# Storing the factors with fewer transfers, v's parts from ScalarE, and sums in pieces of 16 tokens

## The chip, the cores and the metric

The kernel runs on one core of a Trainium2 chip. The metric is the device time of one execution in microseconds (us). A span is the time from the first to the last instruction of the program in a profiled execution.

## The reference

Eight batches, eight heads, 576 tokens, head size 64, 32 memories a head. The first half compresses keys and values into memories and attends to them; the second routes the 128 best tokens of each batch through a two-layer network.

```python
a = phi - np.max(phi, axis=2, keepdims=True)          # phi: (b, h, s, m), softmax over the tokens s
a = np.exp(a)
a = a / (np.sum(a, axis=2, keepdims=True) + 1e-09)
k_m = np.einsum('bhsm,bhsd->bhmd', a, k)
v_m = np.einsum('bhsm,bhsd->bhmd', a, v)
scores = (1.0 / np.sqrt(q.shape[-1])) * np.matmul(q, k_m.transpose(0, 1, 3, 2))
attn = np.exp(scores - np.max(scores, axis=-1, keepdims=True))
attn = attn / (np.sum(attn, axis=-1, keepdims=True) + 1e-09)
x = np.matmul(attn, v_m)                              # then laid out as (b, s, 512)
scores = np.einsum('bsd,d->bs', x, w_gate)
out = x.copy()
for b in range(B):
    top_idx = np.argpartition(-scores[b], capacity)[:capacity]   # capacity = 128
    xe = x[b, top_idx]
    ye = np.maximum(xe @ w1, 0.0) @ w2                # 512 -> 1024 -> 512
    g = 1.0 / (1.0 + np.exp(-scores[b, top_idx]))
    out[b, top_idx] = x[b, top_idx] + g[:, None] * ye
```

Which tokens are chosen depends on the scores, so much of the arithmetic is carried out more exactly than fp32 instructions alone would do it: numbers are split into a high and a low part.

## The kernel before

**Groups and the softmax.** Heads are taken in 16 groups (batch, four heads): 4 x 32 memories fill the 128 partitions, and the 576 tokens lie along the free dimension. `softmax` runs one group through some 29 instructions of VectorE and 16 of ScalarE on tiles of 128 x 576; a `yield` cuts it into steps. Two channels (`ch` 0 and 1) with buffers of their own take turns through the first eight groups; the other eight run on channel 0 alone. Its last part, `keys`, transposes the factors a on TensorE (line 314), has ScalarE copy them out (316), splits them into `hi` and `lo` on VectorE (320, 322), stores both parts to a DRAM tensor `aparts` (325: eight transfers from POOL's queue, one for each part and head), and multiplies them with k (331).

**v.** `split_v` loads v of a group (whole groups in the first phase, halves later; line 291), splits it on VectorE (294, 296) and stores both parts to DRAM, `vparts`, each twice (298, from POOL's queue).

**The sums.** v_m is summed token by token in a fixed order. `all_sums` works on sets of two batches (four groups): a piece of `T` = 18 tokens is loaded back from DRAM with `load_rows`, one transfer for v (344) and four for a (351, one for each of the four heads), all from SyncE's queue, so that 32 partitions hold the combinations of parts; then 18 x 4 small products accumulate in PSUM (382). Three buffers `v_rows` and `a_rows` rotate. A set is 32 pieces, and there are four sets. The first piece of a set waits until the schedule's turn is at least five past that in which the set's last group was made (line 367).

**Attention and network.** `attention(b)` centres the memories (`centre`), computes scores (490) from a loaded q (108), exp and tanh of them (476 to 479), the attention sum (548), divides (552), adds the mean over the memories (555: on POOL while softmaxes are still under way, on VectorE after that), computes gate scores (520 to 525), stores x twice (560, 564), ranks the tokens (`rank`, 601) and gathers the chosen rows (630). `ffn` is the network (654, 664) and scatters the result (671). The next batch's q is loaded between scores and attention sum (683).

**The order.** The instruction order is written out by a loop over turns at the end of the function. Each turn takes one step of a softmax; every fourth turn (every second, once attentions run) one step of `split_v`; 7 steps of the sums before attentions run, 10 beside them and softmaxes, 12 after; one step of each live attention; and two of the network. A step of the sums is two tokens. Each engine executes its own instructions strictly in this order, and SyncE, ScalarE and POOL issue their transfers in it too. When channel 1 is through, its buffers are freed and new pools are opened, among them `vio2` for v's halves with one buffer.

Of the kernel before, what the change touches and what calls it, by code (L numbers as in the profile page):

```python
# [39 lines left out]
def kernel(  # L40
# [26 lines left out]
    F = w1.shape[1]  # L67
    KD, KF = D // P, F // P
    SET = 2
    T = 18  # L70
    scale = 1.0 / Dh ** 0.5
    out_flat = out.rearrange("b s d -> (b s) d")

# [28 lines left out]
    def load_k(i, ch):  # L102
        ks[i] = exs[ch].tile([PT, NC, D // NG], F32, name="kb")
        nc.sync.dma_start(out=ks[i], in_=k[groups[i]])
# [82 lines left out]
    def softmax(i, ch):  # L187

        ex = exs[ch]

        def t(name, dtype=F32):

            return ex.tile([P, NC * P if name in WIDE else S], dtype, name=name)[:, :S]

        r = phis.pop(i)
        less_mx = ex.tile([P, 1], F32, name="mx")
        nc.vector.tensor_scalar(out=t("den"), in0=r, scalar1=-1.0, scalar2=None, op0=ALU.mult,
                                op1=ALU.min, accum_out=less_mx)
        nc.scalar.activation(r, r, AF.Identity, bias=less_mx)
        q = t("q", I16)  # L200
        act(q, r, LOG2E)
        yield
        for ln2 in (LN2_HI, LN2_LO):
            stt(out=r, in0=q, scalar=-ln2, in1=r, op0=ALU.mult, op1=ALU.add)

        rh, rl = t("rh", I16), t("rl")
        act(rh, r, 2.0 ** 11)
        num, den = t("num"), t("den")
        act(num, r, SQ[0], SQ[1], AF.Square)
        act(den, r, EXP_Q[2] * UP, EXP_Q[1] * UP)  # L210
        ends = t("lo"), t("big")
        act(ends[0], rh, -0.2734375 * UP * GRID, UP)
        act(ends[1], rh, UP * GRID / 4, EXP_P[1] * UP)
        yield
        stt(out=num, in0=num, scalar=SQ[2], in1=r, op0=ALU.add, op1=ALU.mult)
        act(num, num, 1.0, EXP_P[2] * UP)
        stt(out=rl, in0=rh, scalar=-GRID, in1=r, op0=ALU.mult, op1=ALU.add)

        def near(val, f, end):


            low = t("low")
            stt(out=low, in0=val, scalar=-f * UP, in1=r, op0=ALU.add, op1=ALU.mult)
            stt(out=low, in0=rl, scalar=f * UP, in1=low, op0=ALU.mult, op1=ALU.add)
            tt(out=val, in0=end, in1=low, op=ALU.add)

        yield
        load_k(i, ch)
        near(den, -0.2734375, ends[0])
        dh = t("dh", I16)  # L230
        act(dh, den, FINE)
        near(num, 0.25, ends[1])
        vh = t("vh", I16)
        act(vh, num, GRID)
        y0 = t("y0", I16)
        act(y0, r, 1.0, 14 * LN2, AF.Exp)
        inv = t("rl2")
        act(inv, r, INV[0], INV[1], AF.Exp)
        act(inv, inv, 1.0, INV[2] - 9 * LN2, AF.Exp)
        yield  # L240


        lo, big, low = t("lo"), t("big"), t("low")
        tt(out=low, in0=num, in1=rl, op=ALU.mult)
        stt(out=lo, in0=num, scalar=GRID, in1=vh, op0=ALU.mult, op1=ALU.subtract)
        tt(out=lo, in0=lo, in1=rh, op=ALU.mult)
        tt(out=big, in0=vh, in1=rh, op=ALU.mult)
        tt(out=low, in0=low, in1=lo, op=ALU.add)
        stt(out=num, in0=big, scalar=UP, in1=low, op0=ALU.add, op1=ALU.add)
        yield  # L250

        dl, p = t("lo"), t("big")
        stt(out=dl, in0=den, scalar=FINE, in1=dh, op0=ALU.mult, op1=ALU.subtract)
        tt(out=p, in0=y0, in1=dh, op=ALU.mult)
        tt(out=num, in0=num, in1=p, op=ALU.subtract)
        tt(out=dl, in0=y0, in1=dl, op=ALU.mult)
        tt(out=num, in0=num, in1=dl, op=ALU.subtract)
        two_q = t("den", I32)
        yield
        act(two_q, q, UP, 127 * UP, AF.Relu)  # L260
        tt(out=num, in0=num, in1=inv, op=ALU.mult)
        tt(out=num, in0=num, in1=y0, op=ALU.add)
        sm = ex.tile([P, 4], F32, name="sm")
        e = num
        stt(out=e, in0=num, scalar=FINE, in1=two_q.bitcast(F32),
            op0=ALU.mult, op1=ALU.mult, accum_out=sm[:, 0:1])

        nc.vector.tensor_scalar_add(sm[:, 0:1], sm[:, 0:1], 1e-9)
        nc.vector.reciprocal(sm[:, 1:2], sm[:, 0:1])
        nc.vector.tensor_single_scalar(sm[:, 2:3].bitcast(I32), sm[:, 0:1].bitcast(I32), -4096,  # L270
                                       op=ALU.bitwise_and)
        nc.vector.tensor_sub(sm[:, 3:4], sm[:, 2:3], sm[:, 0:1])
        nc.vector.tensor_scalar_mul(sm[:, 2:3], sm[:, 2:3], -1.0)
        a0 = t("vh", F16)
        nc.scalar.activation(a0, e, AF.Copy, scale=sm[:, 1:2])  # L275
        yield
        for part in (2, 3):
            stt(out=e, in0=a0, scalar=sm[:, part:part + 1], in1=e, op0=ALU.mult, op1=ALU.add)
        stt(out=e, in0=e, scalar=sm[:, 1:2], in1=a0, op0=ALU.mult, op1=ALU.add)  # L279
        soft[i] = e  # L280
        yield
        yield from keys(i, ch)

    def split_v(some, pool, cuts):

        n = 4 * S * Dh // P
        for b, g in some:
            for x0 in range(0, n, n // cuts):
                x = slice(x0, x0 + n // cuts)
                vb = pool.tile([P, n // cuts], F32, name="vb")  # L290
                nc.sync.dma_start(out=vb, in_=v[b, g, :, x])
                yield
                hi = pool.tile([P, n // cuts], F32, name="vhi")
                nc.vector.tensor_single_scalar(hi.bitcast(I32), vb.bitcast(I32), -4096,
                                               op=ALU.bitwise_and)
                nc.vector.tensor_sub(vb, vb, hi)  # L296
                for vp, src in enumerate((vb, hi)):
                    nc.gpsimd.dma_start(  # L298
                        out=vparts[b, g, :, vp].rearrange("w r s d -> w (r s d)")
                                               .rearrange("w (p x) -> p w x", p=P)[:, :, x],  # L300
                        in_=src.unsqueeze(1).to_broadcast([P, 2, n // cuts]))
                yield
# [3 lines left out]
    def keys(i, ch):  # L306
# [13 lines left out]
        nc.vector.tensor_single_scalar(hi.bitcast(I32), aS.bitcast(I32), -4096,  # L320
                                       op=ALU.bitwise_and)
        nc.vector.tensor_sub(lo, aS, hi)  # L322
        for part, src in enumerate((lo, hi)):
            for h in range(4):
                nc.gpsimd.dma_start(  # L325
                    out=aparts[h, b, g, part].rearrange("(c p) m -> p c m", p=PT),
                    in_=src[:, :, h * M:(h + 1) * M])
        km = bank([P, 2, 2 * M])
        for rr in range(2):
            for c in range(NC):  # L330
# [3 lines left out]
        for u in range(2):  # L334
            part = slice(u * Dh, (u + 1) * Dh)
            nc.scalar.activation(kbd[b][part, 2 * g:2 * g + 2, u * M:(u + 1) * M],  # L336
                                 km[part, :, u * M:(u + 1) * M], AF.Copy)

    accs = [accp.tile([P, 512], F32, name=f"acc{i}") for i in range(2 * SET)]

    def load_rows(k, st, ch):
# [4 lines left out]
            in_=vparts[some].rearrange("b g t w r s d -> (b g t w r) (s d)")  # L346
                [:, ch * T * Dh:(ch + 1) * T * Dh])
        for h in range(4):
            src = aparts[h, some].rearrange("b g t s m -> (b g t) (s m)")
            src = src[:, ch * T * M:(ch + 1) * T * M]  # L350
            nc.sync.dma_start(  # L351
                out=a_rows[k % 3][2 * h::8, h].rearrange("p s m -> p (s m)").bitcast(F32),
                in_=src.unsqueeze(1).to_broadcast([4 * SET, 2, T * M]))

    def all_sums():
# [7 lines left out]
        def load_some(end):  # L363
            while len(loaded) < min(end, len(pieces)):
                st, ch = pieces[len(loaded)]

                if not all(turn >= made.get(i, turn) + 5
                           for i in range(st * SET * NG, (st + 1) * SET * NG)):
                    break
                load_rows(len(loaded), st, ch)  # L370
# [156 lines left out]
    def attend(b, general):  # L527
        eT, tg = eTs[b % 2], tgs[b % 3]
        row, rest = mean[b]
        for c0 in range(0, NT, 2):  # L530
# [5 lines left out]
                                     rhs=heads_of, start=True, stop=True)  # L536
            if working:
                yield
            rd = step.tile([P, 2, H], F32, name="rd")[:, :cols]
            nc.vector.tensor_scalar(out=rd.rearrange("p c (g h) -> p c g h", g=2), in0=den,  # L540
                                    scalar1=float(M), scalar2=1e-9, op0=ALU.add, op1=ALU.add)
# [2 lines left out]
            for c in range(cols):  # L544
                o = bank([P, D])
                nc.tensor.matmul(out=o, lhsT=ones3, rhs=rest, start=True, stop=False)
                for g in range(2):
# [4 lines left out]
                nc.vector.tensor_mul(x[:, c].rearrange("p (h d) -> p h d", d=Dh),  # L552
                                     o.rearrange("p (h d) -> p h d", d=Dh),
                                     rd[:, c].unsqueeze(2).to_broadcast([P, H, Dh]))
            (nc.gpsimd if working else nc.vector).tensor_add(  # L555
                x, x, row.unsqueeze(1).to_broadcast([P, cols, D]))
            yield
            score(tg[:, c0:c0 + cols, 1], x, cols)
# [117 lines left out]
    def attention(b, general=False):  # L676
# [2 lines left out]
        yield from (scores_less_max if general else scores)(b)  # L679
        for j in range(2):  # L680
            yield
            if not general and b + 1 < B:
                load_q(b + 1, j)
        yield from attend(b, general)
        yield
        yield from rank(b)
# [66 lines left out]
    while True:  # L753
# [6 lines left out]
        if working and next(working[0], working) is working:  # L760
            finish(working[1])
            working.clear()
        if working and turn % (2 if attend_all else 4) == 1:
            next(working[1], None)
        for _ in range(steps()):
            next(sums, None)
        if attend_all is None and set(order[1]) <= set(made):
# [4 lines left out]
                ctx.enter_context(tc.tile_pool(name=name, bufs=2 - (name == "one"),  # L772
                                               reuse_waits="tile"))
                for name in ("step", "work", "one"))
            vio = ctx.enter_context(tc.tile_pool(name="vio2", bufs=1, reuse_waits="tile"))
            working[1] = split_v(groups[two + 1:], vio, 2)
            for j in range(2):
                load_q(0, j)
# [58 lines left out]
```

## Time and profile before

| | us |
|---|---|
| median of three runs | 911.14 (907.17 to 918.13) |
| the profiled execution's own time | 899.93 |
| its span | 898.1 |
| PE, DVE, ACT, POOL busy | 584.2, 611.5, 295.3, 234.9 |
| mean granted TensorE clock | 0.822 |

PE is TensorE, DVE VectorE, ACT ScalarE, POOL GpSimd, SPq SyncE's queue, which only issues transfers and is never counted as busy. A busy time is the union of an engine's instructions. In the view of groups and lines, `xN` is a count, then busy us and mean ns of one, then the idle time of the engine ahead of them and what ended it. In the view of waits, a line reads: who waited, for whom, us in total, times, longest. In the view of one line's instructions, three durations in ns are shortest, median and longest.

The engines by 40 equal slices of the span, in tenths:

```
PE   0122322556764646695847889867889989888794
DVE  4899888857874765779789685979845333537820
ACT  3434434324441513332433624343331310332130
POOL 7033311330220432151423314232511010112200
DMA  6367936876857786788554778664256566123300
```

### The profile page before, as it was taken

Reading aid. Unit: us, or ns where it says so; the run is one execution under the profiler, and the core shown is the slowest. Engines: PE = TensorE matmul, PEld = TensorE weight load, DVE = VectorE, ACT = ScalarE, POOL = GpSimd, SP = SyncE. Lnnn points to the kernel's source line nnn. Section 1 sums busy time; section 2 is a strip of 40 time slices with the busy share of each in tenths; the row PEclk is TensorE's granted clock in tenths of the full one; section 3 lists DMA queues with packets and bytes.
Section 4 is the critical chain, followed back from the end, with each engine's and each line's share of the span. In section 5 each row is a group of like instructions: output and inputs, shape, how many; then the busy total and the mean of one; then the engine's idle time right before and its main releaser. Section 6 shows DMA issues by size and latency. Waiting matters only on the chain. (4 is left out here: it accounts for less than half of the span.)

```text
span 898.1 us, 25253 instructions
## 1 busy us (share of the span) xinstructions
PE 584.2 (65%) x10738; PEld 427.7 (48%) x10738; DVE 611.5 (68%) x1117; ACT 295.3 (33%) x578; POOL 234.9 (26%) x349
## 2 busy tenths in 40 slices
PE   0122322556764646695847889867889989888794
PEld 0012222456653535574714557555556577544441
DVE  4899888857874765779789685979845333537820
ACT  3434434324441513332433624343331310332130
POOL 7033311330220432151423314232511010112200
PEclk9999999757585776886667979985899977989597
DMA  6367936876857786788554778664256566123300
GB/s 169 144 198 271 312 124 204 274 250 176 253 154 241 231 259 186 254 289 254 181 186 139 221 210 256 201 191 138 71 171 195 181 202 204 58 77 117 117 25 15
DMA packets 61944, 166.10 MB, mean 185 GB/s; under 512 B 11136, under 2 KB 21376, under 8 KB 61824
## 3 DMA queue, kind: packets, MB, share of 16 engines
q1 hardware_dynamic: 40096, 94.14, 34.8%
q0 software_dynamic: 21728, 70.27, 23.7%
q8 instruction: 87, 1.43, 0.7%
q14 instruction: 33, 0.27, 0.1%
HBM read 96.21 MB, written 68.16 MB: 183 GB/s over the span
## 5 line engine op out<-in xcount | busy, mean ns | idle before, releaser
L382 PE MATMUL acc<-a_rows,v_rows 32*64 32x128 f32 x9216 | 214.3, 253 | 127.8 <-DMA a_rows<-aparts 121.4
L382 PEld LDWEIGHTS acc<-a_rows,v_rows 32*64 32x64 f32 x9216 | 193.5, 162 | 170.4 <-issue 83.0
L314 PE MATMUL bank<-ident,num 128*96 128x128 f32 x96 | 21.3, 386 | 104.4 <-DVE num L279 99.4
L331 PE MATMUL bank<-lo,kb 96*128 96x64 f32 x384 | 64.5, 345 | 20.0 <-ACT lo L316 20.0
L331 PEld LDWEIGHTS bank<-lo,kb 96*128 96x128 f32 x384 | 62.7, 257 | 25.5 <-ACT lo L316 22.4
L325 POOL DMA_DIRECT2D aparts<-low x64 | 46.9, 740 | 104.8 <-DVE low L322 89.7
L298 POOL DMA_DIRECT2D vparts<-vb x23 | 16.9, 735 | 217.8 <-DVE vb L296 217.8
L654 PE MATMUL bank<-w_sb,xeT 128*128 128x512 f32 x128 | 69.8, 679 | 4.9 <-ACT xeT L645 3.2
L314 PEld LDWEIGHTS bank<-ident,num 128*96 128x96 f32 x96 | 15.4, 178 | 108.8 <-issue 88.4
L664 PE MATMUL bank<-w_sb,hT 128*128 128x512 f32 x128 | 60.8, 609 | 0.0
L548 PE MATMUL bank<-vbd,eT 128*128 128x256 f32 x160 | 58.3, 499 | 0.0
L552 DVE TENSOR_TENSOR xj<-bank,rd 128x512 f32<-128x512 f32 x40 | 27.5, 688 | 32.9 <-PE bank L548 32.4
L601 DVE SCALAR_TENSOR_TENSOR cmp<-row,tg,wide 128x576 bf16<-128x576 f32 x40 | 32.5, 814 | 24.0 <-ACT row L587 23.1
L325 POOL DMA_DIRECT2D aparts<-big x64 | 46.5, 734 | 3.8 <-DMA vparts<-vhi 3.7
L548 PEld LDWEIGHTS bank<-vbd,eT 128*128 128x128 f32 x160 | 34.1, 236 | 16.0 <-issue 12.1
L654 PEld LDWEIGHTS bank<-w_sb,xeT 128*128 128x128 f32 x128 | 25.3, 215 | 30.6 <-issue 22.1
L275 ACT ACTIVATE vh<-num,sm 128x576 f16<-128x576 f32 x16 | 12.4, 776 | 78.2 <-DVE sm L270 63.1
L555 POOL TENSOR_TENSOR xj<-xj,mean 128x1024 f32<-128x1024 f32 (+1 forms) x11 | 23.6, 2147 | 49.5 <-DVE xj L552 41.6
L479 DVE SCALAR_TENSOR_TENSOR eT<-es,th 128x288 f32<-128x288 f32 x32 | 14.4, 450 | 31.9 <-ACT th L477 31.9
L664 PEld LDWEIGHTS bank<-w_sb,hT 128*128 128x128 f32 x128 | 22.5, 189 | 25.9 <-issue 24.4
L336 ACT ACTIVATE kbd<-bank 64x64 f32<-64x64 f32 x32 | 7.0, 218 | 83.5 <-PE bank L331 83.3
L560 POOL DMA_DIRECT2D out<-xj x24 | 16.3, 678 | 66.8 <-DVE xj L555 63.8
(149 smaller groups left out, 1155.8 us busy)
## 6 DMA issues: line engine op xcount, KB each, us to landing
v_rows<-vparts SPq DMA_DIRECT2D x128, 288.0 KB
a_rows<-aparts SPq DMA_DIRECT2D x512, 36.0 KB
vparts<-vb POOLq DMA_DIRECT2D x9, 1152.0 KB, 5.5
vparts<-vhi POOLq DMA_DIRECT2D x9, 1152.0 KB, 8.7
kb<-in_k SPq DMA_DIRECT2D x16, 576.0 KB
qb<-in_qT SPq DMA_DIRECT2D x16, 576.0 KB
out<-xj POOLq DMA_DIRECT2D x16, 512.0 KB, 4.1
xs<-xj POOLq DMA_DIRECT2D x16, 512.0 KB, 4.3
```

Source lines behind the costliest of these rows:

```text
L298: nc.gpsimd.dma_start(out=vparts[b, g, :, vp].rearrange("w r s d -> w (r s d)") .rearrange("w (p x) -> p w x", p=P)[:, :, x], in_=src.unsq ...
L314: nc.tensor.transpose(out=tp[:, c], in_=a[:, (c0 + c) * PT:(c0 + c + 1) * PT], identity=ident)
L325: nc.gpsimd.dma_start(out=aparts[h, b, g, part].rearrange("(c p) m -> p c m", p=PT), in_=src[:, :, h * M:(h + 1) * M])
L331: nc.tensor.matmul(out=km[:, rr], lhsT=kb[:, c, rr * P:(rr + 1) * P], rhs=aS[:, c, rr * 2 * M:(rr + 1) * 2 * M], start=(c == 0), stop=(c = ...
L382: nc.tensor.matmul(out=accs[i][:Dh, :P].rearrange("p (h m) -> p h m", m=M), lhsT=vr[p, s], rhs=ar[p, :, s], start=(ch == 0 and s == 0), st ...
L548: nc.tensor.matmul(out=o[:, g * 4 * Dh:(g + 1) * 4 * Dh], lhsT=eT[:, g, (c0 + c) * P:(c0 + c + 1) * P], rhs=vbd[b % 3][:, g], start=False, ...
L552: nc.vector.tensor_mul(x[:, c].rearrange("p (h d) -> p h d", d=Dh), o.rearrange("p (h d) -> p h d", d=Dh), rd[:, c].unsqueeze(2).to_broadc ...
L555: (nc.gpsimd if working else nc.vector).tensor_add(x, x, row.unsqueeze(1).to_broadcast([P, cols, D]))
L560: nc.gpsimd.dma_start(out=out[b, c0 * P:c0 * P + (cols - 1) * P + n].rearrange("(c p) d -> p c d", p=n), in_=x[:n])
L601: nc.vector.scalar_tensor_tensor(out=cmp, in0=row, scalar=g, in1=wide[:, off:off + S], op0=ALU.is_equal, op1=ALU.mult, accum_out=equal[:, ...
L654: nc.tensor.matmul(out=ps[:n], lhsT=xeT[:, d, :n], rhs=w1_sb[:, d, f0:f0 + 512], start=(d == 0), stop=(d == KD - 1))
L664: nc.tensor.matmul(out=ps[:n], lhsT=hT[:, f, :n], rhs=w2_sb[:, f], start=(f == 0), stop=(f == KF - 1))
```

## The change

It has these parts:

- A group's factors are stored by two POOL transfers, one for each part, in place of eight; `aparts` gets a layout in which a token block of 96 and a head are outer dimensions. The stores stand after the products with k in the text.
- A piece of the sums has 16 tokens in place of 18, since a piece must now lie inside a block of 96 tokens.
- v's parts are stored from ScalarE's queue, one step after VectorE has split them; v's halves get a second buffer; `split_v` takes a step in every third turn in the first phase, and in two of three later.
- The mean is added by VectorE throughout.
- k is loaded one step of the softmax later; the next batch's q is loaded inside the attention sum; the rows of a set are loaded four turns, not five, after its last group.

```diff
-    T = 18
+    T = 16
+    assert PT % T == 0
...
         yield
-        load_k(i, ch)
         near(den, -0.2734375, ends[0])
...
         yield
+        load_k(i, ch)
 
         dl, p = t("lo"), t("big")
...
                 nc.vector.tensor_sub(vb, vb, hi)
+                yield
                 for vp, src in enumerate((vb, hi)):
-                    nc.gpsimd.dma_start(
+                    nc.scalar.dma_start(
                         out=vparts[b, g, :, vp].rearrange("w r s d -> w (r s d)")
...
         nc.vector.tensor_sub(lo, aS, hi)
-        for part, src in enumerate((lo, hi)):
-            for h in range(4):
-                nc.gpsimd.dma_start(
-                    out=aparts[h, b, g, part].rearrange("(c p) m -> p c m", p=PT),
-                    in_=src[:, :, h * M:(h + 1) * M])
         km = bank([P, 2, 2 * M])
...
+        for part, src in enumerate((lo, hi)):
+            nc.gpsimd.dma_start(
+                out=aparts[b, g, part].rearrange("c h p m -> p (c h) m"),
+                in_=src.rearrange("p c (h m) -> p (c h) m", m=M))
...
         for h in range(4):
-            src = aparts[h, some].rearrange("b g t s m -> (b g t) (s m)")
-            src = src[:, ch * T * M:(ch + 1) * T * M]
+            src = aparts[some, :, :, ch * T // PT, h].rearrange("b g t p m -> (b g t) (p m)")
+            src = src[:, ch * T % PT * M:(ch * T % PT + T) * M]
...
-                if not all(turn >= made.get(i, turn) + 5
+                if not all(turn >= made.get(i, turn) + 4
...
             if working:
                 yield
+            if c0 == 0 and not general and b + 1 < B:
+                for j in range(2):
+                    load_q(b + 1, j)
...
-            (nc.gpsimd if working else nc.vector).tensor_add(
+            nc.vector.tensor_add(
                 x, x, row.unsqueeze(1).to_broadcast([P, cols, D]))
...
             yield
-            if not general and b + 1 < B:
-                load_q(b + 1, j)
...
-        if working and turn % (2 if attend_all else 4) == 1:
+        if working and (turn % 3 if attend_all else turn % 3 == 1):
             next(working[1], None)
...
-            vio = ctx.enter_context(tc.tile_pool(name="vio2", bufs=1, reuse_waits="tile"))
+            vio = ctx.enter_context(tc.tile_pool(name="vio2", bufs=2, reuse_waits="tile"))
...
-    aparts = nc.dram_tensor("aparts", (4, B, H // 4, 2, S, phi.shape[3]), F32, kind="Internal").ap()
+    aparts = nc.dram_tensor("aparts", (B, H // 4, 2, NC, 4, PT, phi.shape[3]), F32, kind="Internal").ap()
```

## The prediction

> **What bounds the kernel now.** I read the table by stage first, because the page's shares (PE 65%, DVE 68%) average over stages with different limits. The stages are cut where the sums of line 382 begin and end: four sets of 2304 products, one set for every two batches.
>
> ```profile
> 0.00:143.00 143.00, 27.91 (x136) 25.41 (x140) 116.42 (x179) 57.56 (x91) 48.05 (x92) 1.00 0.61 197
> 143.00:282.00 139.00, 77.67 (x2316) 71.37 (x2312) 106.06 (x173) 48.79 (x78) 30.71 (x44) 0.70 0.74 228
> 282.00:420.00 138.00, 91.28 (x2492) 76.24 (x2488) 94.53 (x172) 45.27 (x88) 42.01 (x57) 0.73 0.77 241
> 420.00:482.00 62.00, 37.43 (x283) 25.06 (x279) 49.97 (x100) 20.24 (x44) 20.00 (x25) 0.61 0.52 168
> 482.00:613.00 131.00, 110.27 (x2527) 79.36 (x2523) 101.63 (x188) 55.09 (x109) 44.13 (x55) 0.89 0.72 218
> 661.00:773.00 112.00, 103.32 (x2518) 76.01 (x2510) 43.23 (x88) 15.69 (x36) 14.66 (x23) 0.88 0.62 190
> ```
>
> The columns after the length are PE, PEld, DVE, ACT, POOL busy, granted clock, DMA share, GB/s. Up to 143 us VectorE is busy 81%: the softmax sets the pace. In sets 0 and 1 (143 to 420) no engine is full: PE 56 and 66%, DVE 76 and 68%, ACT a third. In set 2 PE has 84% and DVE 78%; in set 3 PE has 92%, and TensorE carries the rest to the end.
>
> So I asked what PE waits for (second view: waits), and then, since the answer is a load, the issuing queue (third: one line's instructions; fourth: SyncE's timeline).
>
> ```profile
> PE acc L382 <- DMA a_rows<-aparts: 121.4, 49, 8.6
> L351 SPq DMA_DIRECT2D a_rows<-aparts x512: 574/579/2935, 137.8 to 769.2; - x171
> L344 SPq DMA_DIRECT2D v_rows<-vparts x128: 483/502/1804, 110.3 to 766.8; - x128
> 208.76 0.50 SPq L344 DMA_DIRECT2D v_rows<-vparts  x1
> 209.31 2.45 SPq L351 DMA_DIRECT2D a_rows<-aparts  x4
> 211.87 0.50 SPq L344 DMA_DIRECT2D v_rows<-vparts  x1
> 212.41 2.45 SPq L351 DMA_DIRECT2D a_rows<-aparts  x4
> ```
>
> The waits query cut to 143-282 and 282-430 gives 48.2 and 49.3 of those 121.4 us, to 482-613 and 654-773 only 9.3 and 7.1. A piece (18 tokens) takes five issues on SyncE, 0.50 + 4 x 0.58 with gaps between them 3.0-3.1 us from one piece to the next, and in sets 0 and 1 they stand back to back. Added up from the timeline, set 0 (143.7 to 282.3) holds 150 row loads of 103.9 us and 12 other loads of 6.4; set 1 holds 160 of 106.7 and 15 of 9.0. With some 0.1 us of sequencer time between issues only about 12 and 10 us are left in which SyncE waits for PE to give a buffer back. **SyncE's issue queue bounds sets 0 and 1.** In set 2 it waits some 30 us, in set 3 about 10.
>
> The fifth view is line 555, the mean's add, on both engines, and VectorE beside it:
>
> ```profile
> L555 POOL TENSOR_TENSOR xj<-xj,mean x11: 1286/2338/2786, 378.7 to 634.3; 128x1024 f32<-128x1024 f32 x8, 128x512 f32<-128x512 f32 x3
> L555 DVE TENSOR_TENSOR xj<-xj,mean x13: 691/1225/1227, 645.1 to 847.8; 128x1024 f32<-128x1024 f32 x8, 128x512 f32<-128x512 f32 x5
> 577.62 2.79 DVE L262 TENSOR_TENSOR num<-num,y 128x576 f32<-128x576 f32 x1
> DVE prod L520 <- POOL xj L555: 6.7, 2, 4.2
> ```
>
> A VectorE product that takes 0.76 us elsewhere takes 2.79 beside POOL's add at 577.0. Over all eleven adds VectorE's instructions beside them are 15.6 us longer than the shortest of their form.
>
> **What the Trainium skill says.** "DMA: Bandwidth & Descriptors", section "Issuing engines are not separate DMA queues": DMAs from scalar, sync and gpsimd run on the same 16 engines; spreading them saves only the issuing sequencer's time. The trace fits: POOL's stores and SyncE's loads share a DMA share of 0.74-0.77 in sets 0 and 1. So v's stores on ScalarE free POOL, and POOL is busy 26%. "SBUF — State Buffer", section "Who interferes with whom": a VectorE instruction with two SBUF inputs and a GpSimd instruction that reads SBUF exclude each other for the whole instruction. The 2.79 us above agrees.
>
> **The change, part by part.** The sum is made against the profiled execution's own 899.9 us (span 898.1), which lies 11.2 below the median of the three times, 911.1; I add it to the median.
>
> *Pieces of 16 tokens.* A set has 36 pieces in place of 32, so 16 pieces and 80 issues are added on SyncE. The issue price doesn't follow size (0.50 for 288 KB, 0.58 for 36 KB), so I keep it: 4 x 3.0 = 12.0 us a set. Bytes, products and their order are as before. Set 0: 12 less a third for the 12 us of waits for PE, +8 (0 to 12). Set 1: +9 (0 to 12). Set 2: inside the 30 us of waits, 0 (to 4). Set 3: SyncE would need 36 x 3.0 = 108 us and other loads in the 112 us that PE takes: +4 (0 to 10). Together +21 (0 to 38).
>
> *v's parts stored by ScalarE.* 46 issues of 0.72 us (33.5 us) leave POOL, which waits 217.8 us for VectorE at that line and bounds nothing: 0 gained. ScalarE gains 46 issues, not shown here; the nearest row is q's load on SyncE (0.60 us), so 28 us on an engine that is a third busy. More matters in the order of the changed program with its waits named: loads from SyncE and stores from ScalarE draw on the same eight completion semaphores in rotation, and each DMA waits until the one eight places earlier has landed. Before, all of these are SyncE's loads. Now 44 stores each wait for a SyncE load, and 44 SyncE loads each for a store. Behind a store waiting on ScalarE stand the next softmax or exp steps, for which VectorE waits; behind a load waiting on SyncE stand the row loads of the bound stage. v's stores land 5.5 and 8.7 us after issue (whole groups; page section 6), 4.4 and 6.3 (halves); the load that reuses a slot comes some six issues or 3.6 us later, so a pair holds SyncE for up to 2-5 us. Turns counted off the schedule put three whole and about eight half groups into sets 0 and 1: 3 x 5 + 8 x 2.5 = 35 us as a full price. Lower bound 0, if store and load are spaced by the waits that are there anyway; upper 50 with ScalarE's own waits. A stall lets loads in flight land and so shortens the next wait: I take less than half, +15.
>
> *Two stores of a group's factors in place of eight.* POOL issues 2 x 0.73 in place of 8 x 0.73, 4.4 us less in each of 16 groups, on an idle engine. Descriptors stay 128 bytes: 9.4 MB as before. Each store now carries four times as many runs, so its issue may cost 0.73 to 2.9 us. The first row load of a set waited for these stores (27 us at 111, 39 us at 611), but at 660.8 PE came to set 3 without a wait, so an earlier landing buys little: -1 (-5 to +3).
>
> *The mean on VectorE.* 8 x 1.23 + 3 x 0.69 = 11.9 us are added to VectorE; 15.6 us of blocking and 6.7 us of waiting for POOL go: -10.4 on VectorE, which sets the pace in 420-482 and 613-661 and shares it in 482-613. I take -6 (-12 to 0).
>
> *Moved loads and steps.* k's load comes two turns of the schedule later, q's loads later, rows one turn earlier (gate of four turns, not five), v's split has three steps instead of two with a second buffer. SyncE's waits for v's single buffer (34 us) fall into 423-460, before set 2's rows, which PE took up at 480.7 with no wait for them. The turn count drops from 226 to 225 with the same work: 0 (-3 to +3).
>
> Sum: 21 + 15 - 1 - 6 + 0 = **+29**, 929 on the profiled scale and **940** on the median's.
>
> **Rivals.**
> 1. *The slots don't bite, only the pieces do*: 21 - 1 - 6 = +14, 925. For it: before, a load also waits for the one eight back, and those waits are small (5.3 us behind k's loads). Against: stores land later than loads.
> 2. *The other side, faster.* Row issues in sets 0 and 1 cost 36 us more than at their median price (210.6 against 310 x 0.564); one took 2.9 us. If POOL's stores cause this push-back, and it vanishes once they are few and v's are spaced by ScalarE, 36 - 21 = 15 come back, with the blocking -10.4: 911 - 25 = 886. It decides if the mean row issue in sets 0 and 1 drops below 0.60 us from 0.68. Against: the bytes and the sixteen engines are the same.
> 3. *The slots bind fully*: each store in sets 0 and 1 holds ScalarE or SyncE for its landing, +50 in place of +15, and set 2 loses its slack, +10: 911 + 29 + 45 = 985. For it: no engine has slack in order, only in time.
> That the change does not do what it says is out: in the changed order POOL has 32 factor stores, ScalarE 46 v stores, SyncE 144 and 576 row loads.
>
> **How the numbers follow.** Forecast 0.47, rival 1 0.20, rival 2 0.15, rival 3 0.18. Range 898 to 982: it cuts off most of rival 2 and the end of rival 3, and spans the bounds of pieces and slots. A measurement of this kernel tells about 1% from no change. Faster by over 1%: rival 2 and a little of rival 1, 0.17; within 1%: the lower part of rival 1, 0.13; slower 0.70.
>
> **What would show it.** Right: five row issues still cost 3.0 us a piece; set 0 and set 1 lengthen by 10-20 us each; ScalarE or SyncE waits at v's stores; VectorE's 2.3-2.9 us instructions are gone. Wrong: sets 0 and 1 as short as before, PE's 121 us of waits for a_rows fallen, or row issues cheaper at 16 tokens.

## The result, and the profile after

The changed kernel takes **994.43 us** (median of four runs, 988.76 to 998.62) against 910.17 us for the kernel before beside it: a ratio of 1.0907, 95% interval 1.0817 to 1.0997. It is 84 us slower, where 29 were forecast, and lies above the range of 898 to 982. Here and below, a ratio leaves out executions more than 1.5% above the fastest of their kernel, while a median takes in all. The profiled execution is the lowest of the four, 988.76 us (span 986.9). Most line numbers are one higher than before.

The table by stage, cut where each set of sums begins and ends (length, then busy us of PE, PEld, DVE, ACT, POOL, then granted clock, DMA share, GB/s):

```profile
0.00:143.00 143.00, 27.50 (x120) 24.96 (x120) 119.97 (x188) 58.23 (x92) 26.02 (x58) 1.00 0.63 193
143.00:315.00 172.00, 90.01 (x2426) 82.97 (x2427) 103.86 (x168) 48.14 (x78) 9.75 (x10) 0.59 0.65 195
315.00:481.00 166.00, 105.78 (x2497) 87.87 (x2499) 98.93 (x184) 46.65 (x91) 14.10 (x23) 0.65 0.65 191
481.00:521.00 40.00, 33.14 (x111) 21.19 (x106) 36.93 (x74) 18.54 (x40) 8.88 (x12) 0.63 0.75 225
521.00:685.00 164.00, 123.88 (x2600) 88.95 (x2599) 108.37 (x208) 55.42 (x109) 20.92 (x26) 0.79 0.63 188
733.00:863.00 130.00, 111.56 (x2513) 79.98 (x2516) 43.33 (x88) 15.69 (x36) 14.70 (x23) 0.82 0.55 165
```

The prediction's cuts at 282 and 420 us are those of SyncE's row loads; the last products of sets 0 and 1 end at 289.2 and 430.6 us before, and the table below goes by products.

The first set begins when it did (143.2 us, 142.6 before). Between sets 1 and 2 the stage is 10 us shorter (40 against the 50.1 from 430.6 to 480.7 us before); the loss lies in **all four sets**. From the first to the last product of a set, in us, with the mean granted clock, both added up from the traces:

| set | before | after | more |
|---|---|---|---|
| 0 | 146.6 (0.69) | 171.6 (0.59) | 25.0 |
| 1 | 136.9 (0.73) | 164.1 (0.66) | 27.2 |
| 2 | 133.0 (0.89) | 163.3 (0.79) | 30.3 |
| 3 | 112.2 (0.88) | 130.4 (0.82) | 18.2 |

VectorE's busy time fell from 611.5 to 608.7 us and POOL's from 234.9 to 120.6: the work that the change meant to remove is gone, and it wasn't what the sets waited for. The waits of TensorE say what they wait for now (who, for whom, us, times, longest):

```profile
PE acc L383 <- DMA a_rows<-aparts: 195.9, 70, 13.1
```

That wait was 121.4 us in 49 pieces. In sets 0 to 3 it is 91.4, 54.1, 34.8 and 15.7 us, where it was 52.1, 45.4, 9.3 and 7.1. The next thing to read is therefore the queue that loads the rows. These are SyncE's own waits in the changed kernel, those that hold row loads:

```profile
SPq L345 <- PE acc L383: 63.9, 35, 10.2
...
SPq L352 <- DMA vparts<-vb: 29.6, 5, 11.8
SPq L345 <- DMA vparts<-vb: 16.0, 4, 6.7
...
SPq L352 <- DMA vparts<-vhi: 7.7, 7, 2.5
...
SPq L345 <- DMA vparts<-vhi: 2.4, 1, 2.4
```

In the kernel before, row loads wait 1.3 us for v's stores; the last four of these rows come to 55.7 us. The very last, 2.4 us, is a wait for data: the first row load of set 0 needs the v that was stored just ahead of it, and the same wait is there when POOL stores v. The other 53.3 us are waits for something else: each DMA counts up a completion semaphore when it lands, and in this trace ScalarE's stores and SyncE's loads take their turns at the same eight semaphores (numbers 100 to 103 and 106 to 109), while POOL's stores have eight others. A row load that comes to a semaphore waits until the DMA that used it last has landed, here a v store whose data it doesn't need. One such wait in the timeline of the changed kernel (start, duration, engine, line; a wait ahead of an instruction in brackets):

```profile
212.59 14.19 SPq L352 DMA_DIRECT2D a_rows<-aparts  x4
...
215.19 1.36 DVE L297 TENSOR_TENSOR vb<-vb,vhi 128x1152 f32<-128x1152 f32 x1
...
217.26 0.78 ACT L200 ACTIVATE ph<-ph,mx 128x576 f32<-128x576 f32 x1 [2.41 <-DVE den L198]
...
221.16 0.68 ACT L182 ACTIVATE rh<-ph 128x576 int16<-128x576 f32 x1 [2.41 <-DVE ph L205]
...
221.88 0.37 ACTq L300 DMA_DIRECT2D vparts<-vb  x1
222.28 0.48 ACTq L300 DMA_DIRECT2D vparts<-vhi  x1
...
226.88 1.06 SPq L345 DMA_DIRECT2D v_rows<-vparts  x1
```

Four row loads take 14.19 us instead of some 2.45. The fourth is to use semaphore 106, and so is the first v store. SyncE stands still from 214.42, and the store that it waits for **has not been issued yet**: VectorE has v's parts ready at 216.55, but ScalarE comes to the store only at 221.88, behind softmax steps that themselves wait 2.4 us each for VectorE. It lands at 226.19, and only then do the row loads go on. Of the 11.8 us, 4.3 are landing and 7.5 are the store's place in ScalarE's order.

### The profile page after: what moved, and what is told of

Read it like the earlier page. It is cut to its first block, busy times and chain, and to the rows that moved or that the text cites. A ratio compares the mean times of both kernels' runs of the same rounds, so it can differ in the third digit from the quotient of the medians.

```text
span 986.9 us, 25160 instructions
## 1 busy us (share of the span) xinstructions
PE 634.8 (64%) x10738; PEld 464.0 (47%) x10738; DVE 608.7 (62%) x1128; ACT 296.7 (30%) x578; POOL 120.6 (12%) x196
## 5 line engine op out<-in xcount | busy, mean ns | idle before, releaser
L383 PE MATMUL acc<-a_rows,v_rows 32*64 32x128 f32 x9216 | 231.4, 265 | 202.9 <-DMA a_rows<-aparts 195.9
L383 PEld LDWEIGHTS acc<-a_rows,v_rows 32*64 32x64 f32 x9216 | 208.5, 174 | 250.4 <-issue 160.3
L328 PE MATMUL bank<-lo,kb 96*128 96x64 f32 x384 | 70.2, 366 | 15.6 <-ACT lo L318 15.6
L328 PEld LDWEIGHTS bank<-lo,kb 96*128 96x128 f32 x384 | 68.4, 277 | 19.4 <-ACT lo L318 17.7
L336 POOL DMA_DIRECT2D aparts<-low x16 | 19.3, 1209 | 408.8 <-DVE low L324 298.3
L552 PE MATMUL bank<-vbd,eT 128*128 128x256 f32 x160 | 66.0, 554 | 0.0
L552 PEld LDWEIGHTS bank<-vbd,eT 128*128 128x128 f32 x160 | 38.2, 264 | 18.8 <-issue 13.8
L322 DVE TENSOR_SCALAR big<-lo 96x768 int32<-96x768 int32 x16 | 8.8, 552 | 60.7 <-ACT lo L318 60.5
L318 ACT ACTIVATE lo<-bank 96x384 f32<-96x384 f32 x32 | 14.7, 483 | 74.3 <-PE bank L316 74.1
L295 DVE TENSOR_SCALAR vhi<-vb 128x576 int32<-128x576 int32 (+1 forms) x23 | 13.2, 573 | 33.9 <-DMA vb<-in_v 33.8
L536 PEld LDWEIGHTS bank<-heads_of,eT 128*128 128x128 f32 x160 | 30.7, 277 | 5.2 <-issue 3.0
```

Source lines behind the costliest of these rows:

```text
L318: nc.scalar.activation(aS[:, c0:c0 + 3], tp, AF.Copy)
L328: nc.tensor.matmul(out=km[:, rr], lhsT=kb[:, c, rr * P:(rr + 1) * P], rhs=aS[:, c, rr * 2 * M:(rr + 1) * 2 * M], start=(c == 0), stop=(c = ...
L336: nc.gpsimd.dma_start(out=aparts[b, g, part].rearrange("c h p m -> p (c h) m"), in_=src.rearrange("p c (h m) -> p (c h) m", m=M))
L383: nc.tensor.matmul(out=accs[i][:Dh, :P].rearrange("p (h m) -> p h m", m=M), lhsT=vr[p, s], rhs=ar[p, :, s], start=(ch == 0 and s == 0), st ...
L536: nc.tensor.matmul(out=den[:, c, g], lhsT=eT[:, g, (c0 + c) * P:(c0 + c + 1) * P], rhs=heads_of, start=True, stop=True)
L552: nc.tensor.matmul(out=o[:, g * 4 * Dh:(g + 1) * 4 * Dh], lhsT=eT[:, g, (c0 + c) * P:(c0 + c + 1) * P], rhs=vbd[b % 3][:, g], start=False, ...
```

## The experiments

Each is an edit of the kernel before or of the changed one; `T` is the number of tokens in a piece. Differences are medians against the kernel before on the same chip (907.76 to 910.45 us), with the ratio and its 95% interval. Figures by set come from one profiled execution of each kernel, and small ones are uncertain: set 0 differs by 4.8 us between the kernel before and the one with the mean on VectorE alone, whose edit takes effect only at 379 us, after that set.

### The parts one by one

**v's stores put back on POOL, all else as changed.**

```diff
-                    nc.scalar.dma_start(
+                    nc.gpsimd.dma_start(
                         out=vparts[b, g, :, vp].rearrange("w r s d -> w (r s d)")
```

> The changed kernel with one part undone: v's parts are stored from POOL's queue again, all else as changed. Theory of the shared completion slots: in the changed kernel's trace SyncE's row loads wait 55.7 us for v's stores (29.6 + 16.0 + 7.7 + 2.4); without them the median falls from 994 to 940-955, and that wait is gone from SyncE's queue. Rival, the pieces of 16 and their extra issues carry nearly all of the loss: 980-994. Second rival, the two large stores of the factors hold the start of the sets back: 975 or more, with SyncE still waiting at the factors' stores.

948.15 us, 1.044 (1.038 to 1.0501): +38. So ScalarE's stores are worth **46 of the 84 us**. Of SyncE's waits for v's stores at row loads only the wait for data is left:

```profile
SPq L345 <- DMA vparts<-vhi: 2.4, 1, 2.4
```

**Pieces of 16 alone.**

```diff
-    T = 18
+    T = 16
```

> The kernel before with pieces of 16 tokens in place of 18, nothing else. Theory of the fixed issue price: 16 more pieces at 3.0 us, part of it inside waits, +15 to +30, so 925-940, with set 0 and set 1 each 8 to 12 us longer. Rival, pieces carry the whole loss: 970-990. Rival, the issues are hidden: 905-915.

943.38 us, 1.0358 (1.0307 to 1.041): **+33**, where the prediction had +21 and the expectation at most 940 us.

**v's stores on ScalarE alone** (pieces of 18).

```diff
                 for vp, src in enumerate((vb, hi)):
-                    nc.gpsimd.dma_start(
+                    nc.scalar.dma_start(
```

> The kernel before with v's parts stored from ScalarE's queue in place of POOL's, nothing else (no extra step between split and store). Theory of the shared slots: +35 to +55, so 945-965, and SyncE's row loads wait some 40 us or more for v's stores. Rival, only pieces matter: 905-918.

933.09 us, 1.0242 (1.0178 to 1.0306): **+23**, against +15 forecast, and less than the 945 us or more expected here. SyncE's waits at row loads, in this kernel:

```profile
SPq L351 <- DMA vparts<-vb: 27.1, 7, 12.8
...
SPq L351 <- DMA vparts<-vhi: 14.2, 7, 3.3
```

With two smaller rows (3.9 and 1.1 us) that is 46.3 us of waits at v's stores, nearly as much as in the changed kernel; the longest is again over 12 us (219.05 to 231.80, the store issued at 227.48). Here about half of them reaches the end, there nearly all. This kernel isn't quite that part of the change: without the step between split and store, ScalarE itself stands idle ahead of its stores, 41.7 us in all, where in the changed kernel it does so for 3.4. Sets 0 and 1 are 20.9 and 10.3 us longer than before, set 3 is not (108.3).

**The mean on VectorE alone.**

```diff
-            (nc.gpsimd if working else nc.vector).tensor_add(
+            nc.vector.tensor_add(
```

> The kernel before with the mean added by VectorE throughout, nothing else. Theory of the shared port: eleven adds of 1.23 or 0.69 us (11.9 us) come to VectorE, 15.6 us of blocked instructions and 6.7 us of waiting for POOL go, so 899-908. Rival, VectorE's extra work counts and the blocking was beside other waits: 911-922.

902.06 us, 0.9895 (0.9813 to 0.9977): **-8** (the interval is -17 to -2), against -6. The product beside which POOL's add stood took 2.79 us at worst; now the instructions of that line all take the same time (shortest, median, longest ns):

```profile
L262 DVE TENSOR_TENSOR num<-num,y x16: 757/758/759, 33.2 to 626.9; 128x576 f32<-128x576 f32 x16
```

### Why smaller pieces cost more than their issues

**Pieces of 16 with four row buffers.** Room comes from fewer buffers for attention (three `vbd` to two, eight `kbd` to six in turn, three `xe` to two).

```diff
-    T = 18
+    T = 16
...
-    v_rows = [rows.tile([P, T, Dh], F32R, name=f"v_rows{i}") for i in range(3)]
-    a_rows = [rows.tile([P, 4, T, M], F32R, name=f"a_rows{i}") for i in range(3)]
+    v_rows = [rows.tile([P, T, Dh], F32R, name=f"v_rows{i}") for i in range(4)]
+    a_rows = [rows.tile([P, 4, T, M], F32R, name=f"a_rows{i}") for i in range(4)]
```

> Pieces of 16 tokens as in the run of 943, but four buffers of rows in rotation in place of three (64 tokens in flight in place of 48; 18 tokens and three buffers are 54). Space for it comes from two vbd tiles in place of three, six kbd tiles used in turn in place of eight, and two xe tiles in place of three; the fallback for scores of zero, which these inputs don't enter, would find the first two batches' kbd overwritten. Theory of the issue price (SyncE's queue takes 3.0 us a piece, however many are in flight): 930-948, set 3 stays at 125 us or more. Rival, the shorter reach of three small buffers is the loss: 905-920, with SyncE's waits for PE's buffers (77.5 us) cut by half and set 3 back at 112-116 us.

917.30 us, 1.0108 (1.0029 to 1.0186): +10. The 80 extra issues are all still there, and 23 of the 33 us are gone: the issue price alone, at 930 to 948, is out. The three waits of SyncE for PE to give a row buffer back, of pieces of 16 with three buffers, with four buffers, and of the next kernel:

```profile
SPq L344 <- PE acc L382: 77.5, 40, 11.5
```
```profile
SPq L344 <- PE acc L382: 34.1, 30, 9.1
```
```profile
SPq L344 <- PE acc L382: 207.4, 59, 18.8
```

Three buffers of 18 tokens reach 54 tokens ahead of PE, three of 16 reach 48, four of 16 reach 64.

**Pieces of 24 with two buffers**: 48 tokens of reach too, and 160 issues fewer than before.

```diff
-    T = 18
+    T = 24
...
-    a_rows = [rows.tile([P, 4, T, M], F32R, name=f"a_rows{i}") for i in range(3)]
+    a_rows = [rows.tile([P, 4, T, M], F32R, name=f"a_rows{i}") for i in range(2)]
```

> The kernel before with pieces of 24 tokens and two buffers (48 tokens in flight, as with three of 16). 24 pieces a set, so 160 issues fewer than before. Theory of the issue price: 880-905, and PE's waits for rows in sets 0 and 1 fall from 104 us to under 70. Rival, the reach in tokens or in pieces decides: 925-960.

934.81 us, 1.028 (1.0187 to 1.0373): +27. Far fewer issues, and slower nonetheless: what is loaded ahead decides as well as what is issued. Whether tokens or the number of buffers count isn't told apart, since this kernel has two buffers and the one above four.

**80 small loads more on SyncE**, pieces of 18: the issue price by itself, with no change to the pieces.

```diff
+    def load_extra(k):
+        src = w2.rearrange("(t p) f -> p t f", p=P)[:8, 0, :16]
+        nc.sync.dma_start(out=extra[k % 4][0::8], in_=src.unsqueeze(1).to_broadcast([8, 2, 16]))
...
                 load_rows(len(loaded), st, ch)
+                if len(loaded) % 8 < 5:
+                    load_extra(len(loaded))
```

> The kernel before (18 tokens) with 80 small loads added to SyncE's queue, as many as pieces of 16 add, five among every eight pieces: 16 partitions of 64 bytes from a weight, into tiles that nothing reads. Theory of the issue price: an issue of any size costs SyncE 0.58 us, so +20 to +35: 930-945, as with pieces of 16. Rival, the reach of the buffers is the loss, the issues fit into the waits: 908-920.

930.59 us, 1.0266 (1.0184 to 1.0348): +23. One issue takes 0.60 us here, so 48 us in all, of which half reach the end. Sets 0, 1, 2 and 3 are 4, 11, 2 and 4 us longer in the profiled execution (923.72 us, the lowest of four). Issues alone cost 10 us by the run with four buffers and 23 by this one. Four buffers reach further than the kernel before did, which may hide some issues there; so the split of the 33 us is known only as 10 to 23 for issues and the rest for reach.

### The two large stores

**Pieces of 16, new layout, two stores**, and then **the same with eight stores**.

```diff
         for part, src in enumerate((lo, hi)):
-            for h in range(4):
-                nc.gpsimd.dma_start(
-                    out=aparts[h, b, g, part].rearrange("(c p) m -> p c m", p=PT),
-                    in_=src[:, :, h * M:(h + 1) * M])
+            nc.gpsimd.dma_start(
+                out=aparts[b, g, part].rearrange("c h p m -> p (c h) m"),
+                in_=src.rearrange("p c (h m) -> p (c h) m", m=M))
```

> The kernel before with pieces of 16 tokens and the factors stored by two POOL transfers in the new layout; v's stores, the mean and all loads stay as before. In the sum, the changed kernel with v's stores back on POOL (948) less the mean's gain (8) lies 13 above pieces of 16 alone (943). Theory that the two large stores land later (6.8 us after issue, where the eight small ones had 3.5 to 4.3) and hold the start of a set: 950-960. Rival, the moved loads and steps carry those 13 us: 938-948. Second rival, fewer issues on POOL help: 930-937.

```diff
                 nc.gpsimd.dma_start(
-                    out=aparts[h, b, g, part].rearrange("(c p) m -> p c m", p=PT),
+                    out=aparts[b, g, part, :, h].rearrange("c p m -> p c m"),
                     in_=src[:, :, h * M:(h + 1) * M])
```

> Pieces of 16 tokens and the new layout of the factors, but stored by eight POOL transfers a group as before (one for each part and head). With two transfers in this layout the median was 961, with eight in the old layout 943. Theory that the two large transfers are the loss (1.2 us of POOL each and a burst of 288 KB): 938-949. Rival, the layout's addresses are (blocks of 96 tokens and heads outside, so row loads read at a pitch of 288 KiB): 955-967.

961.12 us with two, 1.0588 (1.0505 to 1.067), against 947.53 with eight, 1.0419 (1.0352 to 1.0486). The layout alone is near pieces of 16 alone (943.38; the intervals overlap); **merging eight stores into two costs some 14 us** (15 by the differences from the kernel before) in place of saving one. The timelines show a place for it. With two stores of 288 KB:

```profile
237.59 1.21 POOL L324 DMA_DIRECT2D aparts<-low  x1 [9.09 <-DVE low L322]
...
238.23 3.76 SPq L350 DMA_DIRECT2D a_rows<-aparts  x4
242.09 1.39 SPq L343 DMA_DIRECT2D v_rows<-vparts  x1
```

With eight of 72 KB:

```profile
228.71 2.94 POOL L325 DMA_DIRECT2D aparts<-low  x4 [5.89 <-DVE low L322]
...
228.83 2.58 SPq L351 DMA_DIRECT2D a_rows<-aparts  x4
231.51 0.50 SPq L344 DMA_DIRECT2D v_rows<-vparts  x1
```

While these large stores are under way, SyncE's row issues take longer. Added up from the traces after 140 us, the row issues are 77 us above their median prices of 0.574 and 0.50 us with two stores and 47 with eight; of that extra, 34.5 against 16.0 us stand within 8 us after the issue of a factor store. Pieces of 16 alone have 54, and the changed kernel with v back on POOL, two stores again, 75. That push-back carries the 14 us isn't shown, though. With eight stores and pieces of 16 the figure ranges from 47 to 63 (63 in the kernel with four buffers), the kernel before has 56, and the changed kernel, with two stores, has only 58. The profile with two stores is also of the lowest execution (950.18 us), so the whole 14 us can't be followed in it.

### Moved loads, and why ScalarE's queue costs so much

**Pieces of 16 with the moved loads and steps** (k, q, v's step, rhythm and second buffer, the gate of four turns).

```diff
-    T = 18
+    T = 16
...
-                if not all(turn >= made.get(i, turn) + 5
+                if not all(turn >= made.get(i, turn) + 4
...
-        if working and turn % (2 if attend_all else 4) == 1:
+        if working and (turn % 3 if attend_all else turn % 3 == 1):
...
-            vio = ctx.enter_context(tc.tile_pool(name="vio2", bufs=1, reuse_waits="tile"))
+            vio = ctx.enter_context(tc.tile_pool(name="vio2", bufs=2, reuse_waits="tile"))
```

> Pieces of 16 tokens and all moved loads and steps of the change (k's and q's loads later, rows four turns after the group, v's split in three steps at the new rhythm, second buffer), with v's stores and the mean on POOL and eight stores of the factors as before. Theory that these moves are worth little: the changed kernel with v's stores on POOL (948) less pieces, layout and mean (961 - 8) leaves -5, so 935-945. Rival, they cost, and the layout's 18 us were chance: 950-960.

937.32 us, 1.0324 (1.0251 to 1.0396): 5 us under pieces of 16 alone, with intervals that overlap. The moves may help; no loss is seen.

**Two tiny loads on ScalarE just ahead of each pair of v's stores**, the stores left on POOL, pieces of 18.

```diff
                 nc.vector.tensor_sub(vb, vb, hi)
+                for _ in range(2):
+                    nc.scalar.dma_start(out=extra[count[0] % 4], in_=w2[:P, :16])
+                    count[0] += 1
```

> The kernel before (v's parts stored by POOL) with two small loads, 128 partitions of 64 bytes, issued by ScalarE where v's pair of stores would stand: 46 issues on ScalarE that take their turn in the eight completion slots, but land at once. Theory that the stores hurt because a slot is held until 576 to 1152 KB have landed: 908-918, and SyncE hardly waits for these loads. Rival, any transfer from ScalarE couples the two queues through the order of the slots, whatever its size: 925-936, as with the stores (933).

927.63 us, 1.0176 (1.0105 to 1.0248): +20 by the medians, +16 by the ratio. The profiled execution is the longest of the four, 930.26 us, so its lines are read for their place alone. SyncE's waits:

```profile
SPq L349 <- DMA extra<-in_w: 14.9, 4, 10.1
...
SPq L356 <- DMA extra<-in_w: 6.7, 3, 5.3
```

Loads of 8 KB, which nobody needs, hold the row loads. The longest wait runs from 212.02 to 222.11 us; the loads were issued at 220.55 and 220.92, so nearly all of it is SyncE waiting for ScalarE to arrive. So 16 to 20 of the 23 us of ScalarE's stores alone come with any DMA that stands there, whatever it moves, as far as intervals that overlap can tell. The 46 issues also take 20.4 us of ScalarE's queue, whose effect no run sets apart from that of SyncE's waits.

### What is worth keeping

**The mean on VectorE and k and q loaded from POOL**, which takes 32 issues off SyncE.

```diff
-        nc.sync.dma_start(out=ks[i], in_=k[groups[i]])
+        nc.gpsimd.dma_start(out=ks[i], in_=k[groups[i]])
...
-        nc.sync.dma_start(out=qs[b, j], in_=qT[b, :, :, j * (S // 2):(j + 1) * (S // 2)])
+        nc.gpsimd.dma_start(out=qs[b, j], in_=qT[b, :, :, j * (S // 2):(j + 1) * (S // 2)])
```

> An attempt at a version faster than both: the kernel before with the mean on VectorE, and k's and q's loads issued by POOL in place of SyncE. It takes 32 issues of 0.4 to 0.6 us off SyncE's queue, some 10 in sets 0 and 1, and SyncE's waits for k's and q's buffers (21.8 and 29.7 us) with them; POOL gains 32 issues of some 0.73 us. Theory of the issue bound: 893-902, below the mean alone (902). Rival, the loads arrive late behind POOL's waits for VectorE, and PE or ScalarE waits for them: 905-925.

907.08 us over 14 runs, 0.998 (0.9943 to 1.0017): no gain, and the 8 us of the mean alone are not to be seen either, so that gain, small beside its own interval, may be less than 8. Unloading SyncE by moving loads into another engine's order gave nothing back here.

**The mean on VectorE and the moves, with pieces of 18, eight stores and v on POOL** (the second `vio2` buffer left out).

```diff
+                yield
                 for vp, src in enumerate((vb, hi)):
...
-                if not all(turn >= made.get(i, turn) + 5
+                if not all(turn >= made.get(i, turn) + 4
...
-            (nc.gpsimd if working else nc.vector).tensor_add(
+            nc.vector.tensor_add(
...
-        if working and turn % (2 if attend_all else 4) == 1:
+        if working and (turn % 3 if attend_all else turn % 3 == 1):
```

> An attempt at a version faster than both: the kernel before (18 tokens, stores on POOL) with the mean on VectorE and the change's moved loads and steps, without the second buffer for v's halves, for which there is no space beside 18 tokens. Theory that the gains add (mean -8, moves -6 beside pieces of 16): 890-900. Rival, the moves gain only where SyncE is overfull: 900-906.

**889.87 us** over six runs, 0.9815 (0.977 to 0.9859): faster than both kernels by the parts of the change that leave the pieces and the stores' number and queue alone. Set 0 takes 134.1 us in place of 146.6, and SyncE waits there for row buffers 6.6 us in place of 11.6.

## Why the prediction was wrong, point by point

The runs make a chain from before to after: pieces of 16 (+33), then the layout with two stores (+20, of which 14 are the merging), then the mean, the moves and the factors' stores behind the products with k (-16), then v's stores on ScalarE (+46). It sums to the 84 by construction, but for rounding; a step taken alone may measure otherwise, as the stores on ScalarE do (+23).

**The step that failed** is a part of the sum. Its terms for pieces (+21, where +33 was measured) and for slots (+15, where +23 was measured alone and +46 beside the pieces) were too small: SyncE's waits were taken as slack, each term was priced against the kernel before, and the two were added as if the other weren't there. The two large stores were put at -1 where they cost 14.

**What held.** The direction. The price of an issue: row issues in the changed kernel have a median of 0.575 us for the factors and 0.503 for v, so five make some 3.0 us a piece as before. v's stores left POOL and the sets waited at them. The blocking of VectorE is gone, -8 for -6; "SBUF — State Buffer", section "Who interferes with whom", which stood behind that step, is borne out by the line that went from 2794 to 759 ns at longest. Rival 2 asked for a mean row issue below 0.60 us in sets 0 and 1; it is 0.66 us after and 0.68 before, so that relief never came.

**What held in part** is the bound, SyncE's issue queue. 80 issues more cost 23 us; but 32 fewer gained nothing that can be measured, and 160 fewer, with two larger buffers, were slower. The queue and what it has loaded ahead bound the sets together.

**Pieces, +21 forecast, +33 measured.** The term that failed is "set 2: inside the 30 us of waits, 0; set 3: +4". In the profiled execution of pieces of 16 alone (951.65 us, 8 above its median) sets 0 to 3 are 12.6, 5.7, 11.8 and 19.8 us longer. Of the 30 us, moreover, 11.6 are one wait that begins ahead of set 2's first product. I counted issues and took SyncE's waits for PE as slack into which issues can grow. But that wait is set by the buffers: smaller pieces in as many buffers let SyncE run fewer tokens ahead, so the waits grew, from 62.7 to 77.5 us, in place of shrinking. A fourth buffer cut them to 34.1. In set 3 the idle time of TensorE accounts for 10.0 of the 19.8 us; the other 9.8 are its own busy time (see the clock below).

**Slots, +15 forecast, +46 measured beside the rest.** The mechanism was named rightly and priced wrongly twice. First, "a pair holds SyncE for up to 2-5 us" counts the landing. In the six waits of 4.7 to 11.8 us for v's first store in sets 0 to 2, 42.3 us, the store was issued 0.5 to 7.5 us after SyncE had begun to wait, 20.3 us together: half of the wait is the distance between two engines' places in their orders. Second, "a stall shortens the next wait: I take less than half" was right only for pieces of 18, where 46.3 us of waits cost 23. With pieces of 16 it fell: the price that I halved, 35, is near the 26.1 + 16.6 us of waits at v's stores that sets 0 and 1 show, and those sets are 18.8 and 19.7 us longer than with the stores on POOL, set 2 another 9.7; nothing was made up later. Rival 3, *the slots bind fully*, had just these terms, +50 and +10 in set 2, and with 985 was nearest, though its pieces and its two stores were too cheap; the range up to 982 cut it off at a chance of 0.18. Why 46 and not 23 when pieces are 16 isn't settled by a run: with less reach PE has fewer tokens in hand when SyncE stalls, which fits, but no stall was tried with four buffers.

**Two stores, -1 forecast, +14 measured.** POOL's issue of a large store did come at the low end of the forecast (1.19 us, in place of 0.73 to 2.9). The bound "-5 to +3" looked at POOL's issues and at landing alone; the run with eight stores in the same layout shows that the cost comes with the merging. SyncE's dearer issues beside a large store may be how, but that isn't shown. "DMA: Bandwidth & Descriptors", section "Issuing engines are not separate DMA queues", says that spreading over issuing engines saves only the issuing sequencer's time; this trace agrees that nothing else was saved, and shows more than that: two issuing engines whose DMAs take turns at the same completion semaphores delay each other, by up to 11.8 us at a time.

**Moved loads, 0 forecast**: by the medians -5 with pieces of 16, and -10 beyond the mean's own 8 with pieces of 18, both below the bound of -3. The term looked only at whether the sets' first rows would come earlier; set 0 itself became 12.5 us shorter in the kernel of 889.87 us. The moves do the same beside pieces of 16 (144.4 us against 159.2), so chance is unlikely, but which of them does it, and how, stays open.

**The granted clock wasn't in the sum at all.** PE's busy time rose from 584.2 to 634.8 us with the same products. "TensorE: Matmul & The Clock Gate", section "HAM oscillation — how this bites in real kernels", tells of gaps over about 3.4 us after which PE starts slow again. In set 0 the trace has 8 such gaps before and 9 after; in set 3 it has none in either, and yet 0.88 fell to 0.82. So that rule alone doesn't explain it. In set 3 all six kernels with pieces of 16 and three buffers have 0.81 to 0.84, and TensorE stands idle 17.5 to 20.3 us within the set; all the others have 0.88 to 0.92, and 8.0 to 14.6 us of idle time. So a lower clock goes with more idle time, in the changed kernel all of it in gaps too short for the rule; which brings about which stays open. Of the 19.8 us that set 3 loses with pieces of 16 alone, 9.8 are busy time and 10.0 idle time.

## What to carry to other kernels

Before a DMA is moved to another engine's queue, look for what the two queues share, here completion semaphores in rotation, and price the stall by how far apart the two engines stand in their orders as well as by the transfer's landing time. Price two parts together where both draw on the same reserve, here the tokens loaded ahead. When a piece gets smaller, count bytes or tokens in flight as well as issues: waits for buffers are not slack if the same edit shrinks the buffers. Fewer, larger stores on an idle engine can still make the whole slower.

## What the runs showed of the hardware

- In the changed kernel ScalarE's stores and SyncE's loads take turns at the same eight completion semaphores, so an engine can stand still for a transfer that the other hasn't issued yet: 7.5 of one wait of 11.8 us.
- ScalarE issues a v store in 0.37 us (the first) or 0.48 (the second), half of POOL's 0.72; the cheap issue was of no use:

```profile
L300 ACTq DMA_DIRECT2D vparts<-vb x23: 366/367/421, 34.1 to 639.3; - x23
L300 ACTq DMA_DIRECT2D vparts<-vhi x23: 366/483/1661, 34.5 to 639.7; - x23
```

- 46 tiny loads on ScalarE cost 16 to 20 us of the whole, and 80 tiny loads on SyncE 23.
- A POOL store of 288 KB in runs of 128 bytes takes 1.19 us to issue where a quarter of it takes 0.73, so four in one are 2.5 times cheaper for POOL; the two stores of a group reach DRAM 5.8 and 8.7 us after issue (medians):

```profile
L336 POOL DMA_DIRECT2D aparts<-low x16: 1177/1192/1397, 45.1 to 714.2; - x16
```
```profile
aparts<-low POOLq DMA_DIRECT2D x16, 288.0 KB, 5.8
aparts<-big POOLq DMA_DIRECT2D x16, 288.0 KB, 8.7
```
